# Removing a kernel's own end barrier, and cutting its last weight load 8/4/2 instead of 9/4/1

## Chip, cores, metric

The kernel runs on 1 core of one Trainium2 chip. The metric is the device time of one execution in microseconds (us), and a kernel's time is the median over its runs. Two lengths must be kept apart:

- the **device time**, which is what is reported as the kernel's time;
- the **span** of the profile, from the first to the last instruction of the program itself.

The difference between them, here called the **gap**, is time that the device counts but in which no instruction of the program runs. Each timed run reports both (the span to 0.1 us).

## The reference

One token of a decoder layer: attention over a cache of 65,536 positions (8 key/value heads, 4 query heads each, head size 128), then a gated MLP of width 1,792. Shapes and type (bf16) are fixed. Cut to what matters:

```python
x = A_x                                                    # [1, 1, 512]
h = x + _A_ref(_layernorm(x), A_k_cache, A_v_cache, A_wq, A_wo)
# _B_ref(z): hmid = sigmoid(z @ w_gate) * (z @ w_up);  return hmid @ w_down
h2 = h + _B_ref(_layernorm(h), B_w_gate, B_w_up, B_w_down) # w_down is [1792, 512]
return h2
```

The two caches alone are 268 MB, which is why the kernel is a load stream with arithmetic hung under it.

## The kernel before

SyncE issues all large loads in one queue. w_down comes last, in three pieces of 9, 4 and 1 of the 14 rows that each partition holds, so that TensorE can start on the first rows while the last are still under way:

```python
WD_SPLIT = [(0, 9), (9, 13), (13, 14)]
...
# the loads (SyncE)
src = B_w_down.rearrange("(p r) n -> p r n", p=128)
for i, (r0, r1) in enumerate(WD_SPLIT):
    dma("sp", ..., f"wd{i}", deps if i == 0 else (), f"wd{i}")
...
# the products (TensorE): 4 matmuls for each row r; the first of each piece waits for its load
for i, (r0, r1) in enumerate(WD_SPLIT):
    for r in range(r0, r1):
        for g in range(4):
            op("pe", lambda e, r=r, g=g: e.matmul(ps(YB, 0, 128, 32 * g, 32 * g + 1), ...),
               ["hhT", f"wd{i}"] if r == r0 and g == 0 else (), "y" if last else None)
# four evictions (VectorE and ScalarE), then the 1 KB output (SyncE)
dma("sp", lambda e: e.dma_start(out[0], y_sb[:, :]), "out", [f"ysb{g}" for g in range(4)], "out")
P.at_end = ("out",)
```

At the end every engine branches to a common block "fin". SyncE waits there until the output has landed, and then all five engines meet in a barrier, that is, none goes on until every one has reported (all waiting is done on semaphores, counters that one engine raises and another waits for):

```python
# in Prog.emit
for e, eng in (("sp", nc.sync), ("pool", nc.gpsimd), ("act", nc.scalar), ("dve", nc.vector), ("pe", nc.tensor)):
    ...
    with nc.body(f"prog_{e}", valid_engines=here):
        (hinted if e in HINTED else run)(e, eng)
        nc.br("fin", engines=here)
nc.switch_bb("fin")
for sem, v, _ in (value[d] for d in self.at_end):
    nc.sync.wait_ge(sem, v)
nc.all_engine_barrier(sem_only=True)
```

## Time and profile before

| | before |
|---|---|
| device time, median of the first 3 runs | 661.1 us (661.03 to 661.42) |
| profiled run: device time / span / gap | 661.46 / 659.55 / 1.91 us |
| DMA busy | 9 tenths or more in 39 of 40 slices, 428 GB/s |
| PE, DVE busy | 64%, 53% of the span |
| last bytes of w_down complete | 657.04 us |
| output issued / landed | 658.19 / 659.31 us |

In the profile PE is TensorE (PEld its weight loads), DVE VectorE, ACT ScalarE, POOL GpSimd and SP SyncE; a q behind the name is the engine's sequencer. The page of before: busy times, then DMA in tenths of 40 equal slices of the span.

```profile
span 659.5 us, 6120 instructions
PE 418.8 (64%) x2315; PEld 73.5 (11%) x1547; DVE 349.8 (53%) x439; ACT 43.0 (7%) x114; POOL 3.6 (1%) x17
...
DMA  9999999999999999999999999999999999999997
```

The stream is full from the first slice to the last but one. Only what follows its last bytes is serial, so only that can be shortened by a change like this one. The timeline of before shows this tail (columns: start in us, busy us, engine, line, operation, tiles, count; in brackets the engine's idle time before and what ended it). A DMA line shows only the time of its issue, not its landing.

```profile
655.57 0.87 PEld L831 LDWEIGHTS PS<-ring,hhT 128*1 128x1 bf16 x36 [1.33 <-DVE hhT L826]
655.60 1.88 PE L831 MATMUL PS<-ring,hhT 128*1 128x128 bf16 x56 [1.07 <-DMA ring<-in_B_w_down_dram]
656.78 0.41 PEld L831 LDWEIGHTS PS<-ring,hhT 128*1 128x1 bf16 x20 [0.34 <-DMA ring<-in_B_w_down_dram]
657.53 0.57 ACT L839 ACTIVATE y_sb<-PS 1x128 bf16<-1x128 f32 x2 [4.53 <-PE PS L831]
657.53 0.59 DVE L837 CAST y_sb<-PS 1x128 bf16<-1x128 f32 x2 [2.08 <-PE PS L831]
658.19 0.33 SPq L841 DMA_DIRECT2D out_dram<-y_sb  x1
```

The 20 weight loads from 656.78 are the rows of the second and third piece in one run: TensorE is not stopped between them. From 658.19 on nothing but the output's way remains, and SyncE's own waits tell how it ends (columns: who, for what, us in total, times, longest):

```profile
SPq L212 <- DMA out_dram<-y_sb: 0.8, 1, 0.8
SPq L212 <- PEq L212: 0.2, 1, 0.2
```

SyncE waits 0.8 us for the output and then 0.2 us in the barrier. Single semaphore instructions of the trace show the barrier itself (start and end in us). PE, ACT and DVE report early, SyncE reports when it has the output, GpSimd collects and releases:

```
657.224 657.275  PE    reports
657.634 657.651  ACT   reports
657.674 657.695  DVE   reports
658.990 659.336  SyncE has waited for the output, reports
659.361 659.378  GpSimd has all four reports
659.444 659.461  GpSimd releases
659.486 659.503  SyncE leaves    (ACT 659.507, DVE 659.518, PE 659.549)
```

659.549 is the end of the span; 0.21 us of it lie behind SyncE's wait.

### The profile page before, as it was taken

The page shows a single profiled execution, that of the slowest core. Times are in us where ns is not written, and L with a number is a line of the kernel's source. Part 1 is how long each engine was busy: PE and PEld are TensorE (multiplying, and loading weights), DVE is VectorE, ACT ScalarE, POOL GpSimd, SP SyncE. Part 2 cuts the span into 40 slices and gives each one's busy share as a digit, 9 for nine tenths or more (in the row PEclk, how much of TensorE's full clock was granted, in tenths as well). Part 3 has the DMA queues.
Part 4 walks back from the last instruction along what each step waited for, and adds up shares of the span by engine and source line. Part 5 has one row for each costly group of instructions (what it writes and reads, how often), then busy time and mean ns, then how long its engine had stood idle before and what let it go on. Part 6 is the DMA issues. An engine that isn't in the chain of part 4 may idle for free. (4 is left out here: it accounts for less than half of the span.)

```text
span 659.5 us, 6120 instructions
## 1 busy us (share of the span) xinstructions
PE 418.8 (64%) x2315; PEld 73.5 (11%) x1547; DVE 349.8 (53%) x439; ACT 43.0 (7%) x114; POOL 3.6 (1%) x17
## 2 busy tenths in 40 slices
PE   0598488538566585576865576764855668556846
PEld 0110011001000010010100110000100101001322
DVE  2399865557336665346555374475733565542202
ACT  1100200020000200020000200002000110002001
POOL 1000000000000000000000000000000000000000
PEclk9989689678787696876966678776978769677676
DMA  9999999999999999999999999999999999999997
GB/s 394 433 443 415 443 425 435 443 415 443 417 443 435 423 443 415 443 421 439 441 417 443 415 445 433 425 441 417 443 417 443 439 419 443 415 443 423 437 422 326
DMA packets 10802, 282.34 MB, mean 428 GB/s; under 512 B 1329, under 2 KB 1458, under 8 KB 1842
## 3 DMA queue, kind: packets, MB, share of 16 engines
q1 hardware_dynamic: 10658, 282.33, 99.6%
q10 hardware_dynamic: 144, 0.00, 0.0%
HBM read 282.33 MB, written 0.00 MB: 428 GB/s over the span
## 5 line engine op out<-in xcount | busy, mean ns | idle before, releaser
L431 PE MATMUL PS<-ktw 128*128 128x512 bf16 x1024 | 299.5, 441 | 160.8 <-DVE ktw L511 160.8
L511 DVE STREAM_TRANSPOSE ktw<-ring 128x1024 f32<-128x1024 f32 x256 | 291.7, 1206 | 131.8 <-DMA ring<-in_A_k_cache_dram 131.7
L431 PE MATMUL PS<-ring,PT_sb 128*32 x1024 | 83.5, 455 | 23.7 <-issue 13.2
L431 PEld LDWEIGHTS PS<-ktw 128*128 x256 | 27.0, 106 | 411.3 <-issue 257.7
L565 DVE STREAM_TRANSPOSE PT_sb<-P_sb 128x512 bf16<-128x512 bf16 x32 | 20.2, 684 | 53.6 <-PE PS L602 52.1
L551 ACT ACTIVATE negmax<-PS 128x1 f32<-128x1 f32 x8 | 1.4, 172 | 523.4 <-PE PS L549 523.4
L431 PEld LDWEIGHTS PS<-ring,PT_sb 128*32 x1024 | 25.5, 116 | 80.1 <-issue 75.1
L516 DVE TENSOR_REDUCE M_sb<-PS 128x1 f32<-128x512 f32 x32 | 19.9, 683 | 25.1 <-PE PS L431 25.1
L555 ACT ACTIVATE P_sb<-PS,negmax 128x512 bf16<-128x512 f32 x32 | 21.6, 686 | 0.3
L572 DVE TENSOR_REDUCE lsum<-PS 128x1 f32<-128x4 f32 x8 | 1.3, 162 | 30.8 <-PE PS L570 30.8
L542 PE MATMUL PS<-identf,gm 128*1 128x128 f32 x16 | 3.3, 291 | 16.9 <-DVE gm L540 16.9
L616 DVE TENSOR_TENSOR Lw<-O,blk_of 128x896 bf16<-128x896 bf16 (+1 forms) x2 | 1.4, 681 | 20.7 <-ACT O L606 20.7
L402 PE MATMUL PS<-st,onesf 128*128 128x2 f32 x4 | 1.2, 364 | 16.2 <-DVE st L401 16.2
L431 PE MATMUL PS<-ring,xz 128*8 x32 | 8.4, 427 | 2.3 <-issue 2.3
L599 ACT ACTIVATE po_sb<-PS,rl 128x512 bf16<-128x512 f32 x8 | 5.5, 687 | 53.0 <-PE PS L431 53.0
L431 PE MATMUL PS<-ktw,O 128*1 x26 | 7.6, 462 | 0.0
L549 PE MATMUL PS<-one_f,gmrep 1*128 1x1 f32 x16 | 4.0, 319 | 5.0 <-DVE gmrep L546 5.0
L555 ACT ACTIVATION_READ_ACCUMULATOR P_sb<-PS,negmax 128x1 f32 x32 | 6.5, 203 | 0.0
L602 PE MATMUL PS<-sel_bf,po_sb 128*128 128x4 bf16 x32 | 2.0, 168 | 6.4 <-ACT po_sb L599 6.4
L476 DVE STREAM_TRANSPOSE qt<-qh 32x512 bf16<-32x512 bf16 x1 | 0.7, 699 | 9.8 <-ACT qh L473 9.8
L417 DVE CAST hT<-x_col 128x4 f32<-128x4 bf16 x1 | 0.2, 170 | 10.8 <-DMA x_col<-in_A_x_dram 10.8
L661 DVE COPY yr<-PS 1x512 f32<-1x512 f32 x1 | 0.7, 678 | 8.3 <-PE PS L659 8.3
(82 smaller groups left out, 73.6 us busy)
## 6 DMA issues: line engine op xcount, KB each, us to landing
ring<-in_A_k_cache_dram SPq DMA_DIRECT2D x32, 4096.0 KB, 29.1
ring<-in_A_v_cache_dram SPq DMA_DIRECT2D x31, 4096.0 KB, 26.8
ring<-in_A_wq_dram SPq DMA_DIRECT2D x1, 4096.0 KB, 12.5
ktw<-in_A_wo_dram SPq DMA_DIRECT2D x1, 3584.0 KB, 12.8
ring<-in_A_v_cache_dram SPq DMA_DIRECT2D x1, 3072.0 KB, 13.1
ring<-in_B_w_gate_dram SPq DMA_DIRECT2D x1, 1792.0 KB, 19.0
ring<-in_B_w_up_dram SPq DMA_DIRECT2D x1, 1344.0 KB, 21.8
ring<-in_B_w_down_dram SPq DMA_DIRECT2D x1, 1152.0 KB, 24.8
```

The costliest lines, as they stand in the source:

```text
L431: return e.add_instruction(mybir.InstMatmult(name=nc.get_next_instruction_name(), engine=mybir.EngineType.PE, ins=[rhs, lhsT], outs=[e.low ...
L511: op("dve", lambda e, d=dst, sr=src: e.transpose(d, sr), deps, f"T{b}.{c}", to="T")
L516: op("dve", lambda e, u=u: e.tensor_reduce(M_sb[:, u % 4:u % 4 + 1], ps(u % NS, 0, 512), AX.X, ALU.max), [f"S{b}.{NC - NR + k}"], f"mx{u}" ...
L542: op("pe", lambda e: e.matmul(ps(MISC, 0, 128, 0, 1), lhsT=gm[:, :], rhs=identf[:, :], start=True, stop=True), [f"gm{h}"], f"gmT{h}", to="Q")
L549: op("pe", lambda e: e.matmul(ps(MISC, 128, 129), lhsT=gmrep[0:1, :], rhs=one_f[0:1, 0:1], start=True, stop=True), [f"gmrep{h}"], f"neg{h}")
L551: op("act", lambda e: e.activation(negmax[:, k:k + 1], ps(MISC, 128, 129), AF.Copy, scale=-att_scale), [f"neg{h}"], f"negmax{h}")
L555: op("act", lambda e, b=b: e.activation(P_sb[:, (b % 4) * 512:(b % 4 + 1) * 512], ps(b % NS, 0, 512), AF.Exp, bias=negmax[:, k:k + 1], sca ...
L565: op("dve", lambda e, b=b: e.transpose(PT_sb[:, (b % 4) * 512:(b % 4 + 1) * 512], P_sb[:, (b % 4) * 512:(b % 4 + 1) * 512]), [f"E{b}", f"o ...
L572: op("dve", lambda e: e.tensor_reduce(lsum[:, :], ps(MISC, 132, 136), AX.X, ALU.add), [f"l{h}"], f"ls{h}", to="D")
L599: op("act", lambda e: e.activation(po_sb[:, :], ps(PO, 0, 512), AF.Copy, scale=rl[:, :]), [f"PV{NR * h + NR - 1}", f"rl{h}"], f"po{h}", to ...
L602: op("pe", lambda e, t=t: e.matmul(ps(OX, 0, 4), lhsT=po_sb[:, t * 128:(t + 1) * 128], rhs=sel_bf[:, 8 * t:8 * t + 8:2], start=(t == 0), s ...
L616: op("dve", lambda e: e.tensor_tensor(Lw[i][:, :].rearrange("p (j c) -> p j c", j=n), bass.AP(tensor=O2, offset=j0, ap=[[NQ, 128], [1, n], ...
```

## The change

The intent was to drop a barrier that was taken to guard nothing: SyncE alone has to know that the output is in memory, and the other engines may end when their work is done. The w_down pieces were re-cut as well, to 8, 4 and 2 rows.

```diff
         nc.switch_bb("fin")
         for sem, v, _ in (value[d] for d in self.at_end):
             nc.sync.wait_ge(sem, v)
-        nc.all_engine_barrier(sem_only=True)
...
-    WD_SPLIT = [(0, 9), (9, 13), (13, 14)]
+    WD_SPLIT = [(0, 8), (8, 12), (12, 14)]
```

The order of instructions on each engine is otherwise the same.

## The prediction

> **What bounds the kernel now.** The load stream. The page of before shows the 16 DMA engines at 9 tenths or more in 39 of 40 slices and 428 GB/s over the 659.5 us span (282 MB), while PE is busy 64% and DVE 53%. So nothing before about 650 us is touched. What follows the last bytes of w_down is a serial tail. From the chain of waits, the timeline and the trace's semaphore events:
> - w_down pieces complete at 655.47, 656.73 and 657.04 us (the last of the 16 engines each time, about 0.2 us after the other 15).
> - PE starts piece 2's first row at 656.78 and the last row (piece 3) at 657.16: rows follow each other at 0.107 us without a gap (granted clock 0.50 here), so piece 3's landing (released 657.08) is hidden, just.
> - Evictions 657.53 to 658.13, output issue 658.19 to 658.52, output landed 659.31, SyncE past its wait at 659.34.
> - The kernel's end barrier: GpSimd collects at 659.36, releases at 659.44, all engines are out at 659.50 to 659.55. PE had arrived at 657.28, ACT and DVE at about 657.7 on their sequencers.
> The device time of the profiled run is 661.46, so 1.9 us lie outside the span.
>
> **What the change does.**
> 1. Takes away the end barrier: 659.34 to 659.55, 0.21 us, all of it after the last useful event, so fully on the path. The span should end at SyncE's wait, about 659.34. The order of instructions of every engine is otherwise the same.
> 2. The other four engines reach the runtime's own ending 1.2 to 2 us earlier (after their own last work). [...] part of what each engine does there (the trace has one 8 KB instruction fetch at 659.62 to 660.05, right behind the barrier) may move under the output's wait. It can't gain if that part belongs to SyncE[...]. I expect 0 to 0.6 us, 0.2 as the mean.
> 3. w_down pieces 9/4/1 rows become 8/4/2. Bytes and number of DMAs are the same. Measured rates between landings: 4608-element rows 423 GB/s, 2048-element 409, 512-element about 375 (128 KB in 0.35); so the end of the stream moves by under 0.05 us. The middle piece should land about 0.3 us earlier (656.4), its four rows finish before the last piece lands, and then two rows (2 x 0.107) follow the last landing where one did: estimate, the last row starts at 657.08 + 0.107 = 657.19 against 657.16. Net -0.05 to +0.05 us: nothing.
>
> **Sum.** 661.1 - 0.21 - 0.2 +- 0.05 = 660.7 us, 0.06% faster. This is far within 2%; before's own runs spread 0.4 us.
> Predicted 660.7 us, range 660.1 to 661.3. Faster by over 2%: 0.003; within 2%: 0.994; slower by over 2%: 0.003.
>
> **What the profile would show.** Right: span about 0.2 us shorter with no events of the end barrier; PE ends near 657.3; output issue at 658.2 +- 0.1; output to landing about 1.1 us unchanged; PE waits a little (about 0.2 us) for the third w_down piece, which it did not before; the gap between device time and span stays at 1.7 to 1.9 us. Wrong: the gap grows by what the span loses[...], or the gap falls by over 0.5 us (then the early engines' endings were the larger part).
>
> **What would make it wrong.** Another chip or a slow state with a different stream rate: 0.1% of it is 0.66 us, more than the change itself.

## The result, and the profile after

Ratios are the mean time of one kernel's runs over that of the other's of the same rounds, so they are not quite the ratio of the medians quoted.

| | before | after |
|---|---|---|
| device time, median (lowest to highest) of 6 | 661.34 (661.03 to 661.42) | 660.70 (660.42 to 660.92) |
| ratio | | 0.9991, 95% interval 0.9979 to 1.0004 |
| profiled run: device time | 661.46 | 660.92 |
| span | 659.549 | 659.280 |
| gap | 1.91 | 1.64 (six timed runs: median 1.40, mean 1.46) |

The interval of the ratio includes 1. But the two sets of six do not overlap, and the experiments below repeat the difference. It is 0.64 us between the medians, a thousandth of the time.

The page after: nothing has changed in the stream or in the engines' busy times.

```profile
span 659.3 us, 6111 instructions
PE 418.7 (64%) x2315; PEld 73.3 (11%) x1547; DVE 349.7 (53%) x439; ACT 42.9 (7%) x114; POOL 3.6 (1%) x17
...
DMA  9999999999999999999999999999999999999998
```

The timeline after, of the same tail:

```profile
655.68 0.43 PEld L830 LDWEIGHTS PS<-ring,hhT 128*1 128x1 bf16 x32 [1.27 <-DVE hhT L825]
...
656.50 0.21 PEld L830 LDWEIGHTS PS<-ring,hhT 128*1 128x1 bf16 x16 [0.39 <-DMA ring<-in_B_w_down_dram]
...
657.13 0.10 PEld L830 LDWEIGHTS PS<-ring,hhT 128*1 128x1 bf16 x8 [0.42 <-DMA ring<-in_B_w_down_dram]
657.13 0.28 PE L830 MATMUL PS<-ring,hhT 128*1 128x128 bf16 x8 [0.23 <-DMA ring<-in_B_w_down_dram]
657.46 0.56 ACT L838 ACTIVATE y_sb<-PS 1x128 bf16<-1x128 f32 x2 [4.29 <-PE PS L830]
657.46 0.59 DVE L836 CAST y_sb<-PS 1x128 bf16<-1x128 f32 x2 [1.83 <-PE PS L830]
658.12 0.33 SPq L840 DMA_DIRECT2D out_dram<-y_sb  x1
```

The second piece is used 0.28 us earlier (656.50 against 656.78), and TensorE then stops before the third, which it did not before. SyncE's waits after have lost their second line:

```profile
SPq L211 <- DMA out_dram<-y_sb: 0.8, 1, 0.8
```

The span is 0.27 us shorter in this pair of traces: 0.21 for the exchange, and 0.06 because SyncE had the output that much earlier (it was issued at 658.12 instead of 658.19). The latter is not the pieces' merit but the clock's. The last matmuls of the two traces ran at different granted clocks (PEclk, the third number from the right, the granted TensorE clock as a share of full speed):

Before, from 655.5 to 657.5 us:

```profile
655.50:657.50 2.00, 1.83 (x56) 1.28 (x56) 0.00 (x0) 0.00 (x0) 0.00 (x0) 0.50 0.31 111
```

After, the same stretch:

```profile
655.50:657.50 2.00, 1.29 (x56) 0.74 (x56) 0.17 (x2) 0.04 (x1) 0.00 (x0) 1.00 0.42 160
```

At 0.50 the last matmul started at 657.168 and its evictions at 657.533 (0.365 us later); at 1.00 they were 657.194 and 657.463 (0.269 us). Two more traces part the two causes. From the landing of the last piece to the first eviction it was 0.49 us (9/4/1, before) and 0.48 us (8/4/2, experiment 2 below) at 0.50, and 0.32 us (9/4/1, experiment 1) and 0.38 us (8/4/2, after) at 1.00. The clock record switches between 0.50 and 1.00 after 3 to 34 us each time, at other moments in each trace, so one pair of traces must not be read finer than 0.1 us here.

So the span accounts for 0.2 us of the 0.64. The rest came out of the gap, where no profile line can show it. What follows is about that part.

### The profile page after: what moved, and what is told of

Read it like the earlier page. It is cut to its first block, busy times and chain, and to the rows that moved or that the text cites. A ratio compares the mean times of both kernels' runs of the same rounds, so it can differ in the third digit from the quotient of the medians.

```text
span 659.3 us, 6111 instructions
## 1 busy us (share of the span) xinstructions
PE 418.7 (64%) x2315; PEld 73.3 (11%) x1547; DVE 349.7 (53%) x439; ACT 42.9 (7%) x114; POOL 3.6 (1%) x17
## 4 chain that ended last, share of the span: by engine, by line
DMA 36%; DVE 28%; PE 28%; issue 6%; ACT 1%; SPq 0%; DVEq 0%
DMA ring<-in_A_k_cache_dram 29%; PE PS L430 26%; DVE ktw L510 22%; DMA ring<-in_B_w_down_dram 4%; DVE M_sb L515 3%; DMA x_col<-in_A_x_dram 2%; DVE PT_sb L564 2%; ACT po_sb L598 1%; PE PS L548 1%; PE PS L541 1%; DVE gmj L543 0%; DVE gmrep L545 0%; PE PS L601 0%; PE PS L569 0%; DVE gm L539 0%
```

## The experiments

Three theories were held against each other.

- **A**: only the exchange of the barrier behind the output's wait was saved (0.2 us, all in the span).
- **B**: the other engines now also do part of the ending that follows the program while SyncE still waits, so the gap shrinks too.
- **C**: the pieces gave part of it.

Each kernel is the one before with the edit shown, pieces 9/4/1 unless said otherwise. All results were correct. The gaps are medians over a kernel's timed runs (five, or six where said), from device time and span of each run. The kernel before, timed in the same jobs, had gaps of 1.86 us (9 runs), 1.86 (9) and 1.83 (11) on three chips; its medians were 661.42, 661.36 and 661.23 us.

### 1. The barrier alone is removed

```diff
-        nc.all_engine_barrier(sem_only=True)
```

> Before with the end barrier removed and the pieces left at 9, 4 and 1 rows. Theory A (only the exchange of the barrier after the output's wait was saved): span 0.21 us shorter, gap between device time and span as in before (1.9 us), time 0.2 us shorter. Theory B (the four other engines also do part of the runtime's own ending while SyncE still waits): span 0.21 us shorter and gap smaller by 0.3 to 0.5 us, time 0.5 to 0.7 us shorter, so the whole of the change's 0.64 us. Theory C (the pieces gave part of it): 0.1 to 0.3 us less gain than the change had.

Measured: 660.79 us (660.48 to 661.01) against 661.42 (661.05 to 661.82). Mean span 659.28 against 659.46 us, gap 1.41 against 1.86. The whole gain of the change is there without the new pieces, 0.63 us between the medians: about 0.2 us in the span and 0.45 us in the gap. This is what B said, and A is out.

### 2. The pieces alone

```diff
-    WD_SPLIT = [(0, 9), (9, 13), (13, 14)]
+    WD_SPLIT = [(0, 8), (8, 12), (12, 14)]
```

> Before with the pieces 8, 4 and 2 rows and the end barrier kept. Theories A and B: within 0.1 us of before, gap 1.9 us. Theory C: 0.2 to 0.4 us shorter. In the trace: piece 2 lands about 0.3 us earlier than in before and the last piece at the same distance from the start of the stream.

Measured: 661.45 us (661.35 to 661.58) against 661.42, gap 1.85 against 1.86. C is out. In its trace the second piece landed 0.62 us before the last (656.67 and 657.29), where it was 0.31 us in before (656.73 and 657.04). TensorE had the second piece's rows done and stopped for the third, as the timeline of this kernel shows. In before the last such stop lay ahead of the second piece, at 656.78:

```profile
657.33 0.10 PEld L831 LDWEIGHTS PS<-ring,hhT 128*1 128x1 bf16 x8 [0.23 <-DMA ring<-in_B_w_down_dram]
```

The earlier middle piece was worth nothing here (661.45 against 661.42 us), since the last piece ended the stream in both kernels.

### 3. The barrier put ahead of the wait

```diff
+        nc.all_engine_barrier(sem_only=True)
         for sem, v, _ in (value[d] for d in self.at_end):
             nc.sync.wait_ge(sem, v)
-        nc.all_engine_barrier(sem_only=True)
```

> Before with the two last statements exchanged: first the barrier, then SyncE's wait for the output. The barrier is still executed by all engines, but while the output is under way (it is issued until about 658.5 and lands at 659.3). Theory A (only the exchange behind the output counts): time 0.2 us shorter, gap 1.9. Theory B (early engines): they leave the barrier at about 658.75, 0.5 us before SyncE, so most of the gain: 0.4 to 0.6 us shorter, gap 1.5 to 1.7. If the barrier cost something by being executed at all, it would be slower than the kernel without one by about 0.2 us.

Measured: 660.99 us (660.78 to 661.40), mean span 659.30, gap 1.69. The span is as short as without a barrier (659.28 in experiment 1), so executing the barrier cost nothing here while the output was under way. But the gap fell by only 0.17 us. The trace gives the reason, and it corrects the number expected: SyncE issued the output from 658.138 to 658.465 and executed its next instruction, the report to the barrier, only at 658.949. GpSimd released the others at 659.074 to 659.091, just 0.21 us before SyncE's own last instruction ended at 659.299. The engines were early by little, and the gap shrank by little.

### 4. No barrier, but nobody early

```diff
+        told = self.es.enter_context(nc.semaphore("told"))
         for sem, v, _ in (value[d] for d in self.at_end):
             nc.sync.wait_ge(sem, v)
-        nc.all_engine_barrier(sem_only=True)
+        nc.sync.sem_inc(told, 1)
+        nc.tensor.wait_ge(told, 1)
+        nc.scalar.wait_ge(told, 1)
+        nc.vector.wait_ge(told, 1)
+        nc.gpsimd.wait_ge(told, 1)
```

> Before with the barrier replaced by one semaphore that SyncE raises after its wait for the output, and on which the other four engines wait: no exchange, but no early engine either. Span ends some 0.05 to 0.1 us after SyncE's wait. Theory A (exchange): time 0.1 to 0.2 us shorter, gap 1.9. Theory B (early engines): time 0.1 to 0.2 us shorter too, but 0.3 to 0.5 us longer than the kernel without a barrier, since the gap stays at 1.9 us where that kernel's is 1.5.

Measured: 661.26 us (660.88 to 661.54), gap 1.86. In the trace SyncE raised the semaphore at 659.349 and the last engine was past it at 659.429, 0.08 us later instead of 0.21. There is no barrier in this kernel, yet its gap is that of before. So it is not the barrier as such that costs the 0.45 us, but that engines are held to the end.

### 5 to 8. One engine held

The edit is as in 4, with one of the four waits kept: TensorE, ScalarE, VectorE or GpSimd.

```diff
+        told = self.es.enter_context(nc.semaphore("told"))
...
-        nc.all_engine_barrier(sem_only=True)
+        nc.sync.sem_inc(told, 1)
+        nc.tensor.wait_ge(told, 1)      # or nc.scalar, nc.vector, nc.gpsimd
```

TensorE held:

> No barrier, pieces 9, 4 and 1; TensorE alone waits on a semaphore that SyncE raises after its wait for the output; ScalarE, VectorE and GpSimd end at once. Measured so far: gap between device time and span 1.92 us (mean of 9) with all engines held to the end, 1.45 without a hold. If TensorE's own ending is what was on the path [...], the gap is 1.85 to 1.95 and the time 0.4 us longer than without a hold; if another engine's is, the gap stays at 1.4 to 1.5 us; if every late engine costs a little, about 1.55 us.

ScalarE held:

> The same with ScalarE alone held. If ScalarE's ending was on the path: gap 1.85 to 1.95; if not: 1.4 to 1.5; if each engine costs a little: about 1.55 us.

VectorE held:

> The same with VectorE alone held. If VectorE's ending was on the path: gap 1.85 to 1.95; if not: 1.4 to 1.5; if each engine costs a little: about 1.55 us.

GpSimd held:

> The same with GpSimd alone held. If GpSimd's ending was on the path: gap 1.85 to 1.95; if not: 1.4 to 1.5; if each engine costs a little: about 1.55 us.

| held | time, median (range), us | gaps of the five runs, median (range), us |
|---|---|---|
| TensorE | 661.09 (660.68 to 661.63) | 1.59 (1.55, 1.58, 1.59, 2.13, 2.17) |
| ScalarE | 660.82 (660.68 to 660.96) | 1.52 (1.48 to 1.66) |
| VectorE | 660.62 (660.50 to 660.85) | 1.44 (1.40 to 1.45) |
| GpSimd | 661.18 (660.89 to 661.44) | 1.88 (1.84 to 2.03) |
| none (experiment 1, other chip) | 660.79 | 1.41 (1.37 to 1.69) |
| all (experiment 4, other chip) | 661.26 | 1.86 (1.78 to 2.14) |

GpSimd alone brings the whole gap back, in every run. Its trace holds, behind SyncE's wait (L213), one instruction of one other engine:

```profile
L213 SPq EVENT_SEMAPHORE  x1: 17/17/17, 659.0 to 659.0; - x1
L214 POOLq EVENT_SEMAPHORE  x1: 17/17/17, 659.0 to 659.0; - x1
```

VectorE costs nothing, ScalarE and TensorE about 0.1 us or a little more, and TensorE had two runs at about 2.15 us. The other kernels with one engine held do not show such runs, but the kernel with all held has one at 2.14 us. GpSimd is the engine with the least work in the program (3.6 us busy; its last instruction of the program proper begins at about 651.5 us), and it is the one whose early end matters.

### 9. GpSimd released 0.3 us before SyncE's end

```diff
+        told = self.es.enter_context(nc.semaphore("told"))
+        nc.sync.sem_inc(told, 1)
         for sem, v, _ in (value[d] for d in self.at_end):
             nc.sync.wait_ge(sem, v)
-        nc.all_engine_barrier(sem_only=True)
+        nc.gpsimd.wait_ge(told, 1)
```

> No barrier, pieces 9, 4 and 1, GpSimd alone held, but only until SyncE is past the issue of the output, about 0.3 us before SyncE's own end. Theory B in its sharp form (GpSimd's own ending needs 1.9 us from its release, SyncE's 1.45 us): gap 1.9 - 0.3 = about 1.6 us. If being held costs a fixed amount: 1.9 us. If only the order of arrival counts (GpSimd before SyncE): 1.45 us.

Measured: 660.90 us (660.64 to 661.10), gap 1.55 (1.53 to 1.60). In the trace GpSimd was past its wait (L214) at 659.038, SyncE past its own (L213) at 659.342:

```profile
L211 SPq EVENT_SEMAPHORE  x1: 17/17/17, 659.0 to 659.0; - x1
L214 POOLq EVENT_SEMAPHORE  x1: 17/17/17, 659.0 to 659.0; - x1
L213 SPq EVENT_SEMAPHORE  x1: 17/17/17, 659.3 to 659.3; - x1
```

This is a dose: GpSimd ends 0.30 us ahead of SyncE instead of just behind it as in experiment 8, and the gap is 0.33 us below that kernel's 1.88 (0.28 us below the 1.83 of before in the same jobs). GpSimd executes one more wait in both kernels, so it is not the added instruction that costs the time, but when it ends. With the others, measured from GpSimd's last instruction to the end of the device time (the gap, plus the distance from GpSimd's last instruction to the end of the span in that kernel's trace):

| kernel | GpSimd ends before the span's end by | gap | sum |
|---|---|---|---|
| before | 0.09 | 1.86 | 1.95 |
| barrier first (3) | 0.21 | 1.69 | 1.90 |
| all held (4) | 0.04 | 1.86 | 1.90 |
| GpSimd held (8) | 0.00 | 1.88 | 1.88 |
| GpSimd until the issue (9) | 0.30 | 1.55 | 1.85 |

The sum is the same within 0.1 us wherever GpSimd is among the late ones. (The gaps are medians and the distances come from one trace each. With the traced run's own gap the sums are 2.00, 1.90, 2.15, 1.88 and 1.86 us; the traced run of experiment 4 was the longest in gap of its five.) From SyncE's last instruction it is about 1.4 us when nobody is held (experiment 1). So the end of the device time is, as far as these runs show, the later of two: about 1.9 us after GpSimd's end, or about 1.4 us after SyncE's. A third term is needed where TensorE is held and GpSimd is not (experiments 5 and 10): there the device time ended about 1.6 us after TensorE's last instruction. (All three include whatever the device time counts ahead of the first instruction.)

### 10. Only GpSimd free

As experiment 4, without the line for GpSimd.

> No barrier, pieces 9, 4 and 1; TensorE, ScalarE and VectorE held until SyncE has the output, GpSimd alone ends early. The converse of holding GpSimd alone. If GpSimd's ending was what the barrier had put on the path: gap about 1.5 us in most runs, at most 1.6. TensorE held alone gave 1.55 to 1.59 in three runs and 2.13 to 2.17 in two: if that belongs to TensorE, some runs here show 2.1 us again; if it was chance, none do.

Measured: 660.94 us (660.81 to 661.21), gaps 1.54, 1.54, 1.57, 1.61 and 1.91, median 1.57. The converse holds in part: with three engines held and GpSimd free, the gap fell by 0.26 us (from 1.83 in the same jobs), where freeing all four took off 0.45, and the time by 0.29 us of 0.63. What is missing in the gap is about what TensorE cost alone in experiment 5 (1.59 us). No run was at the 2.1 us that the expectation held possible. The one at 1.91 us recalls the two with TensorE held, but five runs do not settle whether late endings of TensorE are sometimes longer.

### 11. The wait for the output moved to VectorE

```diff
-            nc.sync.wait_ge(sem, v)
-        nc.all_engine_barrier(sem_only=True)
+            nc.vector.wait_ge(sem, v)
```

> No barrier, pieces 9, 4 and 1, and the wait for the output on VectorE in place of SyncE, so that VectorE is the last engine and SyncE is free from about 658.9 us, 0.3 us earlier. If SyncE's own ending sets the 1.45 us that remain without a barrier, the gap falls to 1.2 to 1.3 us and the time is about 0.2 us shorter than without a barrier (a version that beats both kernels). If VectorE's ending takes as long as SyncE's (held VectorE gave 1.43 us behind its own end), nothing changes: gap 1.4 to 1.5 us.

This was tried as a version that might beat both kernels. Measured: 660.88 us median, with gaps of 1.46, 1.38, 1.45, 2.38 and 2.91; ratio to before 1.0005 (0.9992 to 1.0018). The three usual runs (660.76 to 660.88) equal the kernel without a barrier, so VectorE's ending is about as long as SyncE's and nothing is gained. The two long ones (662.18 and 662.41 us) are of a kind that before shows as well (gaps 2.53 and 3.41 in two of the nine runs beside experiments 5 to 8). Their cause is open.

### 12. Five barriers

```diff
-        nc.all_engine_barrier(sem_only=True)
+        for _ in range(5):
+            nc.all_engine_barrier(sem_only=True)
```

> Before with five end barriers in place of one. One exchange took 0.21 us in the trace, so the span grows by 4 x 0.2 = 0.8 us at most (somewhat less if engines need no SyncE delay in the repeats, 0.6), and the gap stays at 1.9 us: 662.0 to 662.3 us. If a barrier had a cost outside the span, the gap would grow with the number of barriers, to over 3 us.

Measured: 665.61 us median of six (662.95 to 666.12), span 660.8 to 661.2, gaps 1.95, 2.83, 4.31, 5.10, 5.12 and 5.22. This is not what B expected: the mean span grew by 1.6 us over before's in the same jobs, not by 0.8 at most, and the gap did not stay at 1.9. Two things differ. SyncE waited 1.3 us in five exchanges, where it waited 0.2 us in the one of before:

```profile
SPq L213 <- PEq L213: 1.3, 5, 0.3
```

The exchanges: the first ended at 659.439, the fifth at 660.917, so a further barrier costs (660.917 - 659.439) / 4 = 0.37 us, more than the 0.21 us of the single one. A single barrier finds three engines already reported. In a repeated one TensorE reports last, 0.15 us after it left the one before (659.439 to 659.588), and the other 0.22 us follow that report.

The gap: it grew by up to 3.4 us and scattered widely. That it grows with barriers as such is contradicted by experiments 3 and 4, where it depends on who is late. A rival is that five barriers make every engine's program longer, and that fetching instructions then falls behind the end: in this trace the one 16 KB instruction fetch runs from 662.68 to 663.87, 1.76 us after TensorE's last instruction, where it starts 1.0 us after it in before (660.54 to 661.56) and about as late in experiment 4 (660.44 to 661.77, 1.01 us). But in before and in experiment 4 the device time did not wait for the end of this fetch: those runs took 661.46 and 661.54 us in all, less than the fetch's end counted from the first instruction. In experiments 9 and 11 it lies inside the program (from 658.48 and 658.46), and the traces of experiments 1 to 3, 5 to 8 and 10 and of after hold no such fetch at all. No run here separates the two, so the cause of this kernel's long gap stays open. It does not bear on the change, which has one barrier less, not four more.

## Why the prediction was right or wrong

The predicted time was met: 660.7 us. Point by point:

- **The stream bounds the kernel and is untouched: right.** Busy times and rate are the same on both pages, and the large loads take the same time from issue to landing within 0.5 us.
- **The exchange, 0.21 us, fully on the path: right.** The span lost it in the traces, and the mean span fell by 0.18 us in experiment 1.
- **The pieces, -0.05 to +0.05 us: right.** Experiment 2 found 0.03 us between the medians. The step-by-step forecast also held: the second piece landed 0.27 us earlier (656.46 against 656.73), and TensorE waited for the third. That the last row started at 657.18, where 657.19 was forecast, is partly luck: the last landing was 0.05 us later, and the clock was 1.00 instead of 0.50.
- **Step 2, the early engines, "0 to 0.6 us, 0.2 as the mean": the mechanism was right, the size too small.** The size was the author's estimate; no trace showed it. This is the mis-sized term: it measured 0.45 us (gap 1.86 to 1.41 in experiment 1, held engines giving it back in experiment 4). The text listed as a sign of being right a gap of 1.7 to 1.9 us after the change; it was 1.40 (median). The step took all engines' endings to be alike. They are not: GpSimd's ending takes about 0.5 us longer than SyncE's, so in before GpSimd, released 0.04 us ahead of SyncE, was the engine the device time waited for. Two details of the step were off as well. It counted the engines as 1.2 to 2 us early, while GpSimd's last work in after ended at 652.2, 7 us before SyncE's end. And the 8 KB instruction fetch that it named as a part that may move did not move: it starts 0.30 us after the output's landing in before (659.616 after 659.314) and 0.31 us in after (659.553 after 659.246). What did move is not seen in the traces.
- **Two errors cancelled.** The forecast was a fall of 0.4 us from 661.1. The real fall was 0.64 us, but from 661.34: the three first runs of before lay low in its spread.

Experiments 1, 4 and 8 agree in kind (gaps of 1.41 us with no engine held, 1.86 with all held and 1.88 with GpSimd alone held, against 1.83 to 1.86 in before): the end of the device time waits for engines other than SyncE, for GpSimd above all, so the kernel's own barrier added only delay. What fills the gap of about 1.4 us that stays is not shown: the traces hold no program instruction there.

Open: why GpSimd's ending is longer, and TensorE's a little; the occasional gaps above 2 us, with and without the barrier; and the gap of the kernel with five barriers.

## What to carry to other kernels

In this kernel it was enough that one engine waited for the output (SyncE in experiment 1, VectorE in experiment 11): the results stayed correct. Try to let the other engines run into their end, and do not tie an idle engine, such as GpSimd here, to the last event; whether a barrier elsewhere guards something has to be checked there. Look at device time minus span run by run: a change of the ending can be worth more there than in the profile, and an experiment that holds one engine at a time finds the one that counts. And keep the scale in mind: all of it was 0.64 of 661 us, while re-cutting the last load, with the stream full, was worth nothing.

## Figures of single steps, as measured here

- **From an engine's last instruction to the end of the device time**: 1.85 to 1.95 us from GpSimd's when GpSimd was late (the table of experiment 9), about 1.4 us from SyncE's when only SyncE was late (experiment 1), and about 1.6 us from TensorE's when TensorE was late and GpSimd was not (experiments 5 and 10).
- **A barrier of the kernel's own**: 0.21 us behind the last to report when the others had long done so (before, 659.336 to 659.549), 0.37 us for each repeated one (experiment 12).
- **The 1 KB output, issued by SyncE**: 1.12 us from issue to landing in before (658.19 to 659.31), 1.13 us in after (658.119 to 659.246).
- **SyncE after it issued the output**: its next instruction came 0.47 to 0.48 us after the recorded end of the issue (658.516 to 658.990 in before, 658.465 to 658.949 in experiment 3). What fills this time is not shown. The output's semaphore has two updates in the trace of before, at 658.63 and 659.31.
- **A 16 KB instruction fetch** took 1.0 to 1.3 us at the end of some traces (660.54 to 661.56 in before, 660.44 to 661.77 in experiment 4), where the device time did not wait for its end. Whether it caused the gaps of up to 5.2 us with five barriers is not settled.
